# Strassen's scheme for the channel mixing of a hash-attention and MLP-mixer kernel

## The chip, the cores and the metric

The kernel runs on one core of a Trainium2 chip. The metric is the device time of one execution in microseconds. The engines are named as in the profile: PE is TensorE, which multiplies matrices out of SBUF into PSUM (PEld are its weight loads); DVE is VectorE; ACT is ScalarE; POOL is GpSimd; SP is SyncE, which issues most transfers.

## The reference

Attention in which a query sees only the keys of its own hash bucket (6 signs of a projection), then an MLP mixer: first over the tokens, then over the channels.

```python
q_bits = (np.einsum('bhsd,dk->bhsk', q, proj) > 0)      # k_bits likewise
mask = q_bucket[:, :, :, None] == k_bucket[:, :, None, :]
scores = np.where(mask, scale * np.matmul(q, k.transpose(0, 1, 3, 2)), -1000000000.0)
...
attn_out = softmax(scores) @ v                          # (4, 8, 768, 64)
x = attn_out.transpose(0, 2, 1, 3).reshape(4, 768, 512)
h = np.maximum(x.transpose(0, 2, 1) @ w_tok1, 0.0) @ w_tok2     # token mixing, 768 -> 256 -> 768
u = x + h.transpose(0, 2, 1)
h2 = np.maximum(u @ w_ch1, 0.0) @ w_ch2                 # channel mixing, 512 -> 1536 -> 512
return u + h2
```

The four weight matrices come as float64; the rest is float32.

## The kernel before

Three stages run one after the other, with all results of attention and mixing kept in SBUF in one tile, XT: 128 partitions, 4 blocks of 128 channels, 4 x 768 = 3072 tokens. In every stage the instructions of an engine stand in the order of the code (`tc.manual_schedule()`).

**attention** loops over 16 pairs of heads and two halves of 384 queries (class Half). For each half PE makes scores for 6 blocks of 128 keys (L292, product of q and k, and one of the sign bits that sets the mask), ACT takes exponentials out of PSUM (L309), PE multiplies with v (`weigh`, L317), DVE and POOL add the exponentials (`add`, L375 to L382), PE sums over the partitions (L327), DVE takes reciprocals (L329), POOL writes XT (L331). Once for each pair, `hashes` makes the next pair's signs: PE L265 into a small PSUM tile (tag "sm", one buffer, shared with the sums of L327), DVE L270 and L273 out of it, and 8 small transfers. `add_values` (ACT, L256) scales and sums the transposed v, tile vt. In the same loop `weights.some` converts a third of a 768-column piece of float64 weights at a time (class Conversion: ACT L164 and L194, DVE L166, L169, L181 and L195, POOL L184 and L185).

**mixer**, first part, mixes the tokens for each of the 4 batches: PE turns XT (`turn`, L225, copied by ACT), multiplies with w_tok1 (L526, out through ACT) and w_tok2 (L539), and DVE adds the result to XT (L545). Four PSUM buffers serve L526 and L539. After each of the two blocks of `mix1` and after each second channel block of `mix2` stands one call of `weights.one`, a whole conversion step: 16 places in all, for the second half of w_ch1 (tile WC1) and for w_ch2 (tile WC2).

**mixer**, second part, mixes the channels, 512 tokens at a time: `channels(tt)` makes 12 hidden blocks of 128 channels from 4 products each (L555, out through ACT, L560) and 4 output blocks from 12 products each (L565, DVE adds XT at L569, SP sends the result out at L570). `look` reads q and k again and takes their largest magnitude (L577), four pairs after each of four blocks of tokens; `decide` turns the 16 maxima on PE (L586) and leaves a flag. If the flag says that the values are large, a careful version of all stages runs afterwards; with these inputs it doesn't.

## Time and profile before

| | us |
|---|---|
| median of 3 runs | 968.51 (967.71 to 970.48) |
| the profiled execution | 967.04, of it span 965.3 |
| PE / DVE / ACT / POOL busy | 932.7 / 425.4 / 279.8 / 214.3 |
| channel mixing, first to last product | 464.4 to 960.1 |
| mean granted clock of PE | 0.992 of full |

A row of a group of instructions reads: line, engine, operation, tile written <- tiles read, partitions x elements and type, count | busy time in us, mean ns of one | idle time of that engine just before them, and what ended most of it. A row of the timeline begins with the start and the length in us; what stands in brackets is the idle time before it and what ended it.

### The profile page before, as it was taken

To read this page: it belongs to the slowest core of one execution; us is meant where nothing else is said; L and a number is where in the kernel's file an instruction comes from. 1 tells how busy PE (TensorE), PEld (TensorE's weight loads), DVE (VectorE), ACT (ScalarE), POOL (GpSimd) and SP (SyncE) were. 2 spreads that over 40 slices of the span, in tenths; PEclk is the share of its full clock that TensorE was granted. 3 is DMA by queue.
4 is the path that set the end of the run, shared out by engine and by line. 5 is a ranking of instruction groups with operands and counts; after the bars stand their busy time and mean duration, and the time that the engine had idled before them with its cause. 6 is when DMAs were issued, how large, how long until landed. Compare 5 with 4: busy or idle time off the path is not lost.

```text
span 965.3 us, 9061 instructions
## 1 busy us (share of the span) xinstructions
PE 932.7 (97%) x3649; PEld 418.5 (43%) x3649; DVE 425.4 (44%) x351; ACT 279.8 (29%) x390; POOL 214.3 (22%) x120
## 2 busy tenths in 40 slices
PE   5999999999999997999999999999999999999997
PEld 2444444434444443555444444444444444444443
DVE  1689989999899784898100110030020002000000
ACT  3555656565556452442110010011001001100100
POOL 3256345534454333575000000000000000000000
PEclk8999999999999998999999999999999999999999
DMA  5222332332222110441000210030040003000000
GB/s 210 88 101 69 111 123 76 102 124 100 94 75 69 35 58 13 127 131 33 1 0 22 109 43 11 22 141 0 22 148 5 11 32 132 0 33 11 1 12 34
DMA packets 20512, 61.11 MB, mean 63 GB/s; under 512 B 2800, under 2 KB 4208, under 8 KB 20464
## 3 DMA queue, kind: packets, MB, share of 16 engines
q1 hardware_dynamic: 20248, 60.45, 18.2%
q8 instruction: 30, 0.49, 0.2%
q14 instruction: 18, 0.15, 0.1%
q10 hardware_dynamic: 216, 0.02, 0.0%
HBM read 53.48 MB, written 6.29 MB: 62 GB/s over the span
## 4 chain that ended last, share of the span: by engine, by line
PE 82%; DVE 10%; ACT 4%; issue 2%; DMA 1%; SPq 0%; DVEq 0%; ACTq 0%
PE c L565 26%; PE c L555 26%; PE sc L292 14%; PE acc L317 10%; PE sums L327 2%; ACT e L309 2%; DVE tmp L169 2%; PE t L526 2%; PE t L539 2%; DVE tmp L166 1%; DVE den L329 1%; DVE WC L195 1%; DVE esd L381 1%; DVE esd L379 1%; ACT raw L194 1%
## 5 line engine op out<-in xcount | busy, mean ns | idle before, releaser
L555 PE MATMUL c<-XT,WC 128*128 128x512 f32 x576 | 248.2, 592 | 0.0
L565 PE MATMUL c<-r,WC 128*128 128x512 f32 x576 | 248.2, 592 | 0.0
L569 DVE TENSOR_TENSOR o<-c,XT 128x512 f32<-128x512 f32 x24 | 16.6, 690 | 424.2 <-PE c L565 424.2
L309 ACT ACTIVATE e<-sc 128x768 f32<-128x768 f32 x192 | 153.9, 811 | 101.5 <-PE sc L292 100.9
L292 PE MATMUL sc<-qk 64*128 64x384 f32 x768 | 164.7, 508 | 5.6 <-ACT e L309 5.6
L565 PEld LDWEIGHTS c<-r,WC 128*128 128x128 f32 x576 | 109.4, 190 | 137.8 <-issue 137.8
L555 PEld LDWEIGHTS c<-XT,WC 128*128 128x128 f32 x576 | 109.4, 190 | 137.1 <-issue 136.8
L560 ACT ACTIVATE r<-c 128x512 f32<-128x512 f32 x72 | 43.0, 597 | 428.8 <-PE c L555 428.8
L317 PE MATMUL acc<-e,vn 128*64 128x384 f32 x768 | 137.9, 494 | 0.0
L292 PEld LDWEIGHTS sc<-qk 64*128 64x128 f32 x768 | 66.2, 190 | 74.0 <-issue 60.1
L329 DVE RECIPROCAL den<-sums 128x384 f32<-128x384 f32 x32 | 81.8, 2556 | 26.0 <-PE sums L327 26.0
L331 POOL TENSOR_TENSOR XT<-num,den 128x384 f32<-128x384 f32 x32 | 49.1, 1535 | 166.0 <-ACT e L309 150.0
L375 POOL TENSOR_TENSOR esa<-e 128x768 f32<-128x768 f32 x32 | 79.4, 2482 | 19.8 <-ACT e L309 19.8
L317 PEld LDWEIGHTS acc<-e,vn 128*64 128x64 f32 x768 | 49.5, 136 | 78.4 <-issue 69.2
L381 DVE TENSOR_TENSOR esd<-esd,e 128x768 f32<-128x768 f32 x32 | 75.5, 2360 | 1.1
L292 PE MATMUL sc<-bits 64*128 64x384 bf16 x384 | 63.4, 324 | 0.2 <-DMA bits<-g 0.2
L184 POOL TENSOR_TENSOR tmp<-tmp,raw 128x768 f32<-128x768 f32 x20 | 42.2, 2109 | 49.5 <-DVE tmp L181 19.4
L379 DVE TENSOR_TENSOR esd<-esd,e 128x768 f32<-128x768 f32 x32 | 50.1, 1565 | 2.8
L526 PE MATMUL t<-x,W 128*128 128x512 f32 x96 | 44.6, 623 | 2.7 <-DVE den L329 2.7
L539 PE MATMUL t<-W,r 128*128 128x384 f32 x128 | 42.3, 488 | 0.9 <-DVE XT L545 0.9
L185 POOL TENSOR_TENSOR tmp<-tmp 128x768 f32<-128x768 f32 x20 | 39.4, 1972 | 1.6
L577 DVE TENSOR_REDUCE largest<-seen 128x1 f32<-128x1536 f32 x16 | 28.0, 1753 | 26.0 <-DMA seen<-in_qk 25.1
(45 smaller groups left out, 414.0 us busy)
## 6 DMA issues: line engine op xcount, KB each, us to landing
raw<-in_moe_w_ch SPq DMA_DIRECT2D x16, 768.0 KB
seen<-in_qk SPq DMA_DIRECT2D x16, 768.0 KB
qk<-in_qk SPq DMA_DIRECT2D x15, 768.0 KB
vn<-in_v SPq DMA_DIRECT2D x16, 384.0 KB
vt<-in_vT SPq DMA_DIRECT2D x16, 384.0 KB
out<-o SPq DMA_DIRECT2D x24, 256.0 KB
raw<-in_moe_w_tok SPq DMA_DIRECT2D x4, 768.0 KB
bits<-g SPq DMA_DIRECT2D x124, 5.2 KB
```

Source lines behind the costliest of these rows:

```text
L292: nc.tensor.matmul(sc[c][:, i, :HALF], t[rows, 1, P * c : P * c + P], t[rows, 0, qs], start=first, stop=not first,)
L309: nc.scalar.activation(e, sc[c][:, :, :HALF], ACT.Exp, scale=SCALE)
L317: nc.tensor.matmul(acc[D * i : D * i + D, :HALF], vn[:, i, c], e[:, i], start=(c == 0), stop=(c == NR - 1),)
L329: nc.vector.reciprocal(den, ps[:, :HALF])
L331: nc.gpsimd.tensor_tensor(XT[:, hp, at : at + HALF], num, den, op=ALU.mult)
L375: nc.gpsimd.tensor_tensor(self.a, es[0], es[1], op=ALU.add)
L379: nc.vector.tensor_tensor(self.d, self.d, es[5], op=ALU.add)
L381: nc.vector.tensor_tensor(self.d, self.d, es[2], op=ALU.add)
L526: nc.tensor.matmul(ps, W1[:, r, P * j : P * j + P], x[:, r], start=(r == 0), stop=(r == NR - 1),)
L539: nc.tensor.matmul(ps[:, :HALF], r1[:, j, P * cb : P * cb + P], W2[:, j, HALF * half : HALF * half + HALF], start=(j == 0), stop=(j == NJ ...
L555: nc.tensor.matmul(ps, WC1[:, cb, P * t : P * t + P], XT[:, cb, sl], start=(cb == 0), stop=(cb == NCB - 1),)
L565: nc.tensor.matmul(ps, WC2[:, t, P * cb : P * cb + P], r2[t], start=(t == 0), stop=(t == NHT - 1),)
```

## The change

Channel mixing takes 1024 tokens at a time and splits each of its two matrix products into 2 x 2 blocks. Seven products of blocks take the place of eight (Winograd's form of Strassen's scheme); they are made of sums and differences of blocks, all in float32. The sums of the weights (SW1, SW2) are made once by DVE, in four more jobs among the conversion jobs of token mixing (`weight_sums`, `jobs`). The sums of the tokens (T, `inputs`) are made by DVE for each 1024 tokens.

A hidden block of 128 + 128 channels (`hidden`) takes products into four PSUM banks b0 to b3. ACT copies b0, b2 and b3 out (p1, p5, p7), further products are added into the same banks, and DVE and POOL add up the four results, which DVE rectifies in place (L628). All eight banks are two sets of the four. `outputs` does the same with w_ch2, with the differences of the hidden blocks made by DVE in place and in T. `look` stands once behind each hidden block (from the third of the first 1024 tokens), and `decide` behind the last.

In attention, `add_values(0)` moves behind the first scores, `add_values(n + 1)` to the other half, and `hashes(n + 1)` ahead of `weights.some`. The token weights and x0 move to a pool that is closed before channel mixing.

```diff
@@ attention
-        add_values(0)
...
                 now.scores(0)
+                if n == half == 0:
+                    add_values(0)
...
                 now.add(0)
+                if half == 1 and n + 1 < len(pairs):
+                    add_values(n + 1)
                 if half == 0 and n + 1 < len(pairs):
-                    add_values(n + 1)
+                    hashes(n + 1)
                 if n:
                     weights.some(third)
                     third = (third + 1) % 3
-                if half == 0 and n + 1 < len(pairs):
-                    hashes(n + 1)
                 now.weigh(0)
@@ token mixing (mixer becomes tokens; weights.one() becomes job())
+    def weight_sums(w, sums, first, second, low, high):
+        a00, a01 = w[:, first, low], w[:, second, low]
+        a10, a11 = w[:, first, high], w[:, second, high]
+        def early():
+            nc.vector.tensor_tensor(sums[:, 1], a00, a10, op=ALU.subtract)
+            nc.vector.tensor_tensor(a10, a10, a11, op=ALU.add)
+        def late():
+            nc.vector.tensor_tensor(sums[:, 0], a10, a00, op=ALU.subtract)
+            nc.vector.tensor_tensor(sums[:, 2], a01, sums[:, 0], op=ALU.subtract)
+        return [early, late]
...
+            return [
+                *[conversion.one] * (n1 + 1),
+                *weight_sums(WC1, SW1, ...),
+                *[conversion.one] * n2,
+                *weight_sums(WC2, SW2, ...),
+            ]
@@ channel mixing
+        def hidden(s, t, r):
...
+            x.product(0, lambda k: WC1[:, k, low], lambda k: XT[:, k, sl[0]], ks, True)
+            x.product(1, lambda k: WC1[:, KC + k, low], lambda k: XT[:, KC + k, sl[0]], ks, True)
+            x.product(2, lambda k: WC1[:, k, high], lambda k: T[:, k], ks, True)
+            x.product(3, lambda k: SW1[:, 1, k, low], lambda k: T[:, 2 * KC + k], ks, True)
+            p1 = x.copy(0, "p1")
+            nc.vector.tensor_tensor(r[:, 0], x.ps[1], p1, op=ALU.add)
+            p5 = x.copy(2, "p5")
+            x.product(0, lambda k: SW1[:, 0, k, low], lambda k: T[:, KC + k], ks, False)
+            p7 = x.copy(3, "p7")
+            nc.gpsimd.tensor_tensor(p7, p5, p7, op=ALU.add)
+            x.product(2, lambda k: SW1[:, 2, k, low], lambda k: XT[:, KC + k, sl[1]], ks, False)
+            x.product(3, lambda k: WC1[:, KC + k, high], lambda k: T[:, 3 * KC + k], ks, False)
+            u = x.copy(0, "u")
+            nc.vector.tensor_tensor(r[:, 3], p7, u, op=ALU.add)
+            nc.vector.tensor_tensor(r[:, 1], x.ps[2], u, op=ALU.add)
+            nc.vector.tensor_tensor(r[:, 2], x.ps[3], u, op=ALU.add)
+            nc.vector.tensor_scalar(r, r, 0.0, None, op0=ALU.max)
...
+            nc.vector.tensor_tensor(t1, XT[:, low, b], XT[:, low, a], op=ALU.subtract)
+            nc.vector.tensor_tensor(t3, XT[:, high, b], XT[:, low, b], op=ALU.subtract)
+            nc.vector.tensor_tensor(t2, XT[:, high, b], t1, op=ALU.subtract)
+            nc.vector.tensor_tensor(t4, XT[:, high, a], t2, op=ALU.subtract)
...
+        inputs(0)
+        waiting = judge
+        for s in range(B * S // (2 * TT)):
+            rs = []
+            for t in range(HC):
+                r = pool.tile([P, 4, TT], F32, name="r2", tag="r2", bufs=HC)
+                hidden(s, t, r)
+                rs.append(r)
+                if s or t > 1:
+                    look()
+                if waiting and not unseen:
+                    decide()
+                    waiting = False
+            outputs(s, rs)
```

In `outputs`, for each of two output blocks of 128 + 128 channels (m): products of 6 chunks into b0 and b1 of both blocks first, then into b2 and b3 of both, then further ones into b0, b2 and b3. `inputs(s + 1)` stands between the last two groups.

The order of the instructions at the places in question. In the first: DVE in attention, one half with the hashes of the next pair; g are the signs, tmp and raw the conversion, den the reciprocal. Before, and then now:

```order
L382 SCALAR_TENSOR_TENSOR esd<-esd,esa 128x768
L166 TENSOR_SCALAR tmp<-raw 128x768
L169 SCALAR_TENSOR_TENSOR tmp<-raw,tmp 128x768
L270 TENSOR_SCALAR g<-hp 128x384
L273 TENSOR_SCALAR g<-g,bitscale 128x384
L329 RECIPROCAL den<-sums 128x384
```

```order
L383 SCALAR_TENSOR_TENSOR esd<-esd,esa 128x768
L272 TENSOR_SCALAR g<-hp 128x384
L275 TENSOR_SCALAR g<-g,bitscale 128x384
L168 TENSOR_SCALAR tmp<-raw 128x768
L171 SCALAR_TENSOR_TENSOR tmp<-raw,tmp 128x768
L331 RECIPROCAL den<-sums 128x384
```

The two instructions on the signs now stand ahead of the conversion.

The second place is DVE at the end of token mixing, from its last two adds to XT on (t are the banks that PE filled). Before, and then now:

```order
L545 TENSOR_TENSOR XT<-t_3279,XT 128x384
L545 TENSOR_TENSOR XT<-t_3283,XT 128x384
L569 TENSOR_TENSOR o<-c_3371,XT 128x512
L569 TENSOR_TENSOR o<-c_3387,XT 128x512
L569 TENSOR_TENSOR o<-c_3403,XT 128x512
```

```order
L549 TENSOR_TENSOR XT<-t_3291,XT 128x384
L549 TENSOR_TENSOR XT<-t_3295,XT 128x384
L571 TENSOR_TENSOR SW_2867<-WC_2865 128x1536
L681 TENSOR_TENSOR T<-XT 128x1024
L572 TENSOR_TENSOR WC_2865<-WC_2865 128x6x256
L682 TENSOR_TENSOR T<-XT 128x1024
L575 TENSOR_TENSOR SW_2867<-WC_2865 128x1536
L683 TENSOR_TENSOR T<-XT,T 128x1024
L576 TENSOR_TENSOR SW_2867<-WC_2865,SW_2867 128x1536
L684 TENSOR_TENSOR T<-XT,T 128x1024
L617 TENSOR_TENSOR r_3320<-b_3322,p_3333 128x512
```

The four sums of w_ch2 and the first four sums of tokens stand there in turn, ahead of the first hidden block's adds.

The third place is PE around the turning of the maxima (judge). Before it stands ahead of the last 512 tokens, and now between the last hidden block of the last 1024 tokens and their outputs:

```order
L565 MATMUL c_4059<-r_4009,WC_2859 128x512
L586 MATMUL judge<-ident,top 1x128
L555 MATMUL c_4082<-XT,WC_89 128x512 x4
L555 MATMUL c_4089<-XT,WC_89 128x512 x4
L555 MATMUL c_4096<-XT,WC_89 128x512 x4
```

```order
L595 MATMUL b_4251<-T,SW_2866 128x512 x2
L595 MATMUL b_4253<-XT,SW_2866 128x512 x2
L595 MATMUL b_4254<-T,WC_91 128x512 x2
L705 MATMUL judge<-ident,top 1x128
L595 MATMUL b_4293<-r_4070,WC_2865 128x512
L595 MATMUL b_4293<-r_4106,WC_2865 128x512
```

On DVE the maxima of the looks now stand behind the adds of that hidden block:

```order
L626 TENSOR_TENSOR r_4250<-b_4253,u 128x512
L627 TENSOR_TENSOR r_4250<-b_4254,u 128x512
L628 TENSOR_SCALAR r_4250<-r_4250 128x2048
L696 TENSOR_REDUCE largest<-seen 128x1
L703 TENSOR_REDUCE top<-largest 128x1
L707 TENSOR_REDUCE one<-judge 1x1
```

The turning thus comes behind that block's last add, its rectifier and the last look; before, it came behind the last add of the 512 tokens ahead.

## The prediction

> **What bounds the kernel now.** I read the page's busy table, chain and costliest groups first, then the time windows by stage, the table of waits, and the timeline at the places that the edits touch.

> ```profile
> span 965.3 us, 9061 instructions
> PE 932.7 (97%) x3649; PEld 418.5 (43%) x3649; DVE 425.4 (44%) x351; ACT 279.8 (29%) x390; POOL 214.3 (22%) x120
> PE 82%; DVE 10%; ACT 4%; issue 2%; DMA 1%; SPq 0%; DVEq 0%; ACTq 0%
> L555 PE MATMUL c<-XT,WC 128*128 128x512 f32 x576 | 248.2, 592 | 0.0
> L565 PE MATMUL c<-r,WC 128*128 128x512 f32 x576 | 248.2, 592 | 0.0
> ```

> TensorE (PE) is busy 97% of the span and is 82% of the chain that ended last. Channel mixing is 248.2 + 248.2 = 496.4 us of it. The code issues 288 products at each line and the profile shows 576 records, so a 128x512 float32 product is two records: 496.4/576 = 0.862 us. (The mean of 592 ns is a latency; records overlap.) The windows of attention, token mixing and channel mixing (length, then PE, PEld, DVE, ACT, POOL busy, clock, DMA) show the same by stage:

> ```profile
> 60.00:340.00 280.00, 273.73 (x1774) 117.64 (x1772) 254.39 (x187) 163.60 (x224) 130.88 (x67) 1.00 0.27 90
> 380.30:464.40 84.10, 81.30 (x274) 45.57 (x273) 69.05 (x73) 32.10 (x39) 49.13 (x23) 1.00 0.27 85
> 464.40:960.10 495.70, 494.81 (x1154) 218.59 (x1152) 44.98 (x43) 43.00 (x72) 0.00 (x0) 1.00 0.10 38
> ```

> Channel mixing has no gap but one of 0.9 us, and VectorE (DVE) is busy 45 of 496 us: there is cover for sums. In token mixing DVE is at 82%, in attention at 91%.

> **The products.** Per 1024 tokens there are 6 hidden blocks x 7 products x 2 chunks and 2 output blocks x 7 x 6, 168 instead of 192; three times that is 504 instead of 576. 72 x 0.862 = **62.1 us less** on PE.

> **The block sums.** The nearest rows:

> ```profile
> L569 DVE TENSOR_TENSOR o<-c,XT 128x512 f32<-128x512 f32 x24 | 16.6, 690 | 424.2 <-PE c L565 424.2
> L545 DVE TENSOR_TENSOR XT<-t,XT 128x384 f32<-128x384 f32 x32 | 16.3, 550 | 6.1 <-PE t L539 6.1
> L381 DVE TENSOR_TENSOR esd<-esd,e 128x768 f32<-128x768 f32 x32 | 75.5, 2360 | 1.1
> 361.56 0.96 DVE L381 TENSOR_TENSOR esd<-esd,e 128x768 f32<-128x768 f32 x1
> L181 DVE TENSOR_SCALAR tmp<-tmp 128x768 uint32<-128x768 uint32 x12 | 6.7, 560 | 0.4
> L577 DVE TENSOR_REDUCE largest<-seen 128x1 f32<-128x1536 f32 x16 | 28.0, 1753 | 26.0 <-DMA seen<-in_qk 25.1
> L560 ACT ACTIVATE r<-c 128x512 f32<-128x512 f32 x72 | 43.0, 597 | 428.8 <-PE c L555 428.8
> L185 POOL TENSOR_TENSOR tmp<-tmp 128x768 f32<-128x768 f32 x20 | 39.4, 1972 | 1.6
> ```

> 550 ns for 384 and 690 for 512 make 1.09 ns per element: 1.25 us for 1024, 1.81 for 1536 (768 would be 0.97, and L381 shows 0.96 when GpSimd, POOL, is idle; its mean of 2.36 is beside POOL's adds). The rectifier over 2048 is 0.56 x 2048/768 = 1.49.
> A hidden block takes PE 14 x 0.862 = 12.1 us. Under it DVE does 4 x 0.69 + 1.49 + a look at q and k 1.75 = 6.0 us, ScalarE (ACT) 4 copies x 0.6 = 2.4, POOL one add, some 1.4 us. PE adds again into a bank only after its copy: the bank that is written first is reopened after three other products (5 us) against 0.6 for the copy, so no wait. The output stage gives PE 84 x 0.862 = 72.4 us; DVE has 24 subtractions, 12 adds (36 x 0.69 = 24.8) and the next four sums of 1024 (5.0), 30 us. Subtractions of one half are needed 20.7 us (24 products) after their inputs, and 12 pairs take 16.6. I cost all of this at nothing, on PE's cover; without it each hidden block costs PE what DVE needs beyond 12.1 us. SyncE's output transfers come four per pair of blocks instead of one per block; none holds a buffer that is wanted within 12 us.

> **The moves in attention.** add_values(0) leaves the head of ACT's queue; the signs of the hashes (L270) pass the weight conversion in DVE's queue. The table of waits (total, times, longest), the timeline and the GB/s of each microsecond from 0:

> ```profile
> PE sums L327 <- DVE g L270: 6.7, 8, 1.3
> ACT vt L256 <- DMA vt<-in_vT: 14.1, 1, 14.1
> 11.47 0.95 PE L292 MATMUL sc<-bits 64*128 64x384 bf16 x6 [0.19 <-DMA bits<-g]
> 17.16 2.19 ACT L309 ACTIVATE e<-sc 128x768 f32<-128x768 f32 x3
> 18.00 1.65 PE L292 MATMUL sc<-qk 64*128 64x384 f32 x4 [5.58 <-ACT e L309]
> 22.12 0.85 PE L265 MATMUL hp<-qk,projblk 128*32 128x384 f32 x8
> GB/s 0 0 83 353 346 8 0 0 0 0 16 11 16 138 409 424 375 390 418 388 399 438 424 390 412 119 27 5 5 11 5 0 0 184 369 227 6 0 0 0
> 261.17 0.96 DVE L195 SCALAR_TENSOR_TENSOR WC<-raw,tmp 128x768 f32<-128x768 f32 x1 [1.08 <-ACT raw L194]
> 262.05 0.55 DVE L270 TENSOR_SCALAR g<-hp 128x384 bf16<-128x384 f32 x1
> 262.65 0.87 PE L327 MATMUL sums<-esd,ones 128*64 128x384 f32 x4 [1.25 <-DVE g L270]
> ```

> The scores are ready near 12, but ACT stood behind vt until 17.16. Now the three exponentials go first and PE resumes near 12.9. What is late next is q and k of pair 1 for L265: 2 x 384 KB stand ahead of its 768 KB, and the rates from 13 on (138, 409, 424, 375, 390) reach 1.57 MB at 17.6, some 0.7 more to land; L265 starts near 18.3 instead of 22.1. Bounds 0 (later transfers slow it) and 5.7 (it is there at 16.4); I take **3.5 us less**. The 8 waits of 6.7 us are PE waiting for the one small PSUM buffer until L270 has read it, behind L195 or L166 and L169. With L270 ahead they go: behind it now stands the conversion, which the reciprocal waits for, and the reciprocal feeds only POOL, with time. SyncE gets the hash transfers before the weight fetch, which nothing awaits soon. Bounds 3 and 6.7; I take **6.5 less**.

> **Token mixing.** Its slots, 16, now carry 17 jobs (13 conversion steps, four pairs of weight sums). DVE runs late here already:

> ```profile
> 442.23 2.09 DVE L166 TENSOR_SCALAR tmp<-raw 128x768 uint32<-128x768 uint32 x1
> 444.35 2.46 DVE L169 SCALAR_TENSOR_TENSOR tmp<-raw,tmp 128x768 uint32<-128x768 uint32 x1
> 447.32 0.95 DVE L195 SCALAR_TENSOR_TENSOR WC<-raw,tmp 128x768 f32<-128x768 f32 x1
> 448.19 1.94 DVE L545 TENSOR_TENSOR XT<-t,XT 128x384 f32<-128x384 f32 x4
> 448.80 15.75 PE L539 MATMUL t<-W,r 128*128 128x384 f32 x48 [0.74 <-DVE XT L545]
> 464.38 6.17 PE L555 MATMUL c<-XT,WC 128*128 128x512 f32 x14
> ```

> L545's adds stood behind a conversion step (442.23 to 448.2), and PE's next products waited 0.74 us for them at 448.80. Such a step takes 4.5 to 6 us, a pair of sums 3.6 (5.6 beside POOL). The first two pairs (slots 6 and 7) put 9 us in the place of 10.5, so DVE reaches 442 some 2 us earlier; but then two full steps fall between the last adds of L545, where DVE was idle. Walking both queues through the four banks, PE loses about 1.4 us at the last banks. Bounds 0 and 5; I take **1 more**.

> **Entry to channel mixing.** Behind the last L545 add DVE has four weight sums and the first four token sums in turn: 1.81 and 1.25, so that, counted from PE's last product of token mixing and with that add's 0.55, T is complete by quarters at 3.6, 6.7, 9.7 and 12.8 us. PE has two products (3.4 us) that need none; the next three (1.72 each) wait for a quarter each and end at 5.3, 8.4 and 11.4, one that needs none ends at 13.2, and the last at 14.9 instead of 12.1. **2.9 more**; bounds 1 (PE arrives late) and 5 (the last conversion on POOL runs beside them).

> **The judge.** The 16 looks are now one per hidden block, and the last stands behind hidden block 6 of the third pair. PE's transposition (L586 before, L705 now) is queued right behind that block and ahead of all outputs.

> ```profile
> 876.58 0.69 DVE L569 TENSOR_TENSOR o<-c,XT 128x512 f32<-128x512 f32 x1 [9.61 <-PE c L565]
> 877.19 0.16 DVE L584 TENSOR_REDUCE top<-largest 128x1 f32<-128x16 f32 x1
> 877.40 0.27 PE L586 MATMUL judge<-ident,top 128*1 128x128 f32 x1 [0.86 <-DVE top L584]
> 363.73 0.87 PE L327 MATMUL sums<-esd,ones 128*64 128x384 f32 x4 [2.59 <-DVE esd L382]
> 367.33 13.17 PE L526 MATMUL t<-x,W 128*128 128x512 f32 x24 [2.74 <-DVE den L329]
> 384.62 10.46 PE L526 MATMUL t<-x,W 128*128 128x512 f32 x24
> 14.00:15.00 1.00, 0.00 (x0) 0.00 (x0) 0.00 (x0) 0.00 (x0) 0.00 (x0) 0.62 1.05 409
> ```

> PE must wait for the last add 0.69, the rectifier 1.49, the look 1.75, a reduction of 0.16 and four handovers, together 4.3 us, 0.86 of which was paid before: 3.4 more. Such a gap also costs clock: after gaps of 2.59 and 2.74 us the same 24 records took 13.17 instead of 10.46 us, and at the start the granted clock fell to half by 14.2 (0.62 is the mean of that slice), 1.8 us after PE's last work ended at 12.4. I add 2.2 us (half clock for 3.4 to 6.8 us, part of it in the gap). **5.6 more**, bounds 2.5 and 7.
> [...]

> **The end and the sum.** The last add is again one of 512 behind the last product:

> ```profile
> 960.11 0.69 DVE L569 TENSOR_TENSOR o<-c,XT 128x512 f32<-128x512 f32 x1 [9.61 <-PE c L565]
> ```

> From its end, 960.8, to 965.3 lies the transfer, which stays. -62.1 - 3.5 - 6.5 + 1 + 2.9 + 5.6 = -62.6 us: span 965.3 to 902.7. The profiled execution was 967.04 us, 1.7 more than its span and 1.5 below the median of 968.51; 968.5 - 62.6 = **906 us**.

> **Rivals.**
> [...]
> - Attention keeps its time, because the reciprocal or the q and k of pair 1 now make PE wait as long: 906 + 10 = 916. For it: DVE at 91% there. Against it: the PSUM buffer is what the wait names.
> - Token mixing becomes DVE's: its 69 us in 84 grow by 4 pairs x 3.6 = 14.5, at POOL's pace 20; if a half of that lands on PE, 916.
> - DVE bounds the channel blocks in part: at L381's 2.5-fold pace the SBUF-only add and the rectifier make 6.0 into 9.3 us, still under 12.1; but if copies, POOL and DVE run one after the other at each block, 1 to 2 us x 18 are lost: 925 to 940. [...]
> - Slower: the same mechanism beyond its point. 62.6 us over 18 hidden blocks is 3.5 each, so DVE would need 15.6 us per block, 2.6 times my count; it gives 970 and more. No row shows all of DVE's work at that pace.
> - The compiled order could still issue the eighth product: 968. The built program has 504 products, against it.

> **Chances.** Forecast 0.57, clock holds 0.15, attention keeps its time 0.08, token mixing 0.10, partial bound by DVE 0.07, slower 0.02, no effect 0.01. A difference under 0.3% could not be told from none: faster 0.96, same 0.02, slower 0.02. Adding the good ends of the bounds to -62.1 (-5.7, -6.7, 0, +1, +2.5) gives 898; the attention and token cases end at 916 and their sums somewhat above: range 898 to 919, which leaves out the partial bound, slower and no effect.

> **What would show it.** Right: 1008 records of 512 columns at 0.43 us in channel mixing with waits only in its first block and at the judge; PE waiting about 4.3 us for the reduction of the looks, and the clock under 1.0 behind it; no wait of L327 for the signs; first exponentials near 12 us. Wrong: waits of PE on ACT copies or DVE adds in every block, or on token mixing's adds for over 5 us.

## The result and the profile after

The changed kernel takes 907.25 us (median of 4 runs, 905.23 to 907.36) against 968.11 us for the kernel before on the same chip: a ratio of 0.9363, 95% interval 0.9341 to 0.9384. The forecast was 906. Its profiled execution has a span of 905.5 us, 59.8 less than before. The busy line and the same windows by stage as before (the third is channel mixing behind its first hidden block up to the judge, the fourth from there to the last product):

```profile
span 905.5 us, 9108 instructions
PE 873.4 (96%) x3505; PEld 391.5 (43%) x3505; DVE 580.9 (64%) x545; ACT 293.4 (32%) x414; POOL 266.5 (29%) x156
...
60.00:340.00 280.00, 279.05 (x1808) 120.13 (x1806) 258.01 (x189) 167.07 (x228) 134.45 (x68) 1.00 0.25 87
374.28:459.02 84.74, 81.24 (x273) 45.54 (x272) 71.59 (x77) 32.16 (x39) 49.33 (x23) 1.00 0.28 93
473.56:826.12 352.56, 348.65 (x814) 154.09 (x812) 159.92 (x184) 49.23 (x84) 39.70 (x29) 1.00 0.13 46
826.12:900.20 74.08, 74.07 (x169) 32.41 (x169) 25.20 (x37) 4.69 (x8) 7.63 (x6) 0.98 0.07 26
```

PE is still the bound, with 59 us less work. In the attention window its idle time went from 6.3 us to 1.0. In the third window PE is idle for 3.91 us of 352.56, all of it one wait, while DVE is now busy 45% of the window. The table of PE's waits (total, times, longest) names what is left, here without four rows: the first products' wait for projblk (5.9 us, before 6.0), two waits that are as before (1.9 us at L227, 2.7 at L530), and one of 0.7 us of L294 for ACT's exponentials:

```profile
PE hp L267 <- DMA qk<-in_qk: 4.7, 1, 4.7
PE judge L705 <- DVE top L703: 3.9, 1, 3.9
PE sums L329 <- DVE esd L383: 3.4, 3, 2.6
PE t L543 <- DVE XT L549: 1.6, 2, 0.8
PE b L595 <- DVE T L683: 0.9, 1, 0.9
PE b L595 <- DVE T L682: 0.8, 1, 0.8
```

The wait of the sums (L329) for the signs is no longer there. The wait for q and k of the second pair of heads (its index is 1), 4.7 us at the hash products L267, is new. The timeline of the start, with the GB/s of each microsecond from 0:

```profile
12.18 2.21 ACT L311 ACTIVATE e<-sc 128x768 f32<-128x768 f32 x3 [9.94 <-PE sc L294]
20.45 1.51 PE L267 MATMUL hp<-qk,projblk 128*32 128x384 f32 x8 [4.72 <-DMA qk<-in_qk]
21.89 3.71 PE L319 MATMUL acc<-e,vn 128*64 128x384 f32 x12
34.85 0.81 PE L329 MATMUL sums<-esd,ones 128*64 128x384 f32 x4
...
GB/s 0 0 89 375 321 5 0 0 0 4 12 11 16 233 409 200 197 283 332 416 387 408 434 423 418 365 185 73 12 5 0 0 0 55 344 338 49 0 0 0
```

The exponentials do start at 12.18 instead of 17.16, yet the first sums come at 34.85, later than before (34.31, below). Then the entry to channel mixing, the judge, and the last add:

```profile
459.02 3.60 PE L595 MATMUL b<-XT,WC 128*128 128x512 f32 x8
465.44 1.98 PE L595 MATMUL b<-T,SW 128*128 128x512 f32 x4 [0.76 <-DVE T L682]
468.34 1.95 PE L595 MATMUL b<-T,SW 128*128 128x512 f32 x4 [0.91 <-DVE T L683]
473.56 1.88 PE L595 MATMUL b<-XT,WC 128*128 128x512 f32 x4
...
822.97 1.23 DVE L628 TENSOR_SCALAR r<-r 128x2048 f32<-128x2048 f32 x1
824.12 1.75 DVE L696 TENSOR_REDUCE largest<-seen 128x1 f32<-128x1536 f32 x1
825.89 0.17 DVE L703 TENSOR_REDUCE top<-largest 128x1 f32<-128x16 f32 x1
826.12 0.27 PE L705 MATMUL judge<-ident,top 128*1 128x128 f32 x1 [3.91 <-DVE top L703]
826.23 27.61 PE L595 MATMUL b<-r,WC 128*128 128x512 f32 x60
...
900.23 0.69 DVE L673 TENSOR_TENSOR u<-b,u 128x512 f32<-128x512 f32 x1 [4.46 <-PE b L595]
```

The first hidden block takes 473.56 - 459.02 = 14.54 us where the others take 12.02. In front of the judge PE waits for the rectifier, the look and the maxima, 3.15 us of DVE's work in a row. Then the 60 records behind it take 27.61 us, which take 25.91 in the runs without a fall of the clock (below): 0.43 us each, as in the third window, whose clock is 1.00.

### The profile page after: what moved, and what is told of

It is laid out like the page before. It is cut to its first block, busy times and chain, and to the rows that moved or that the text cites. A ratio compares the mean times of both kernels' runs of the same rounds, so it can differ in the third digit from the quotient of the medians.

```text
span 905.5 us, 9108 instructions
## 1 busy us (share of the span) xinstructions
PE 873.4 (96%) x3505; PEld 391.5 (43%) x3505; DVE 580.9 (64%) x545; ACT 293.4 (32%) x414; POOL 266.5 (29%) x156
## 4 chain that ended last, share of the span: by engine, by line
PE 88%; DVE 8%; DMA 1%; ACT 1%; issue 1%; POOL 0%; SPq 0%; DVEq 0%; ACTq 0%
PE b L595 47%; PE sc L294 16%; PE acc L319 13%; PE t L530 4%; PE sums L329 2%; PE t L543 2%; PE hp L267 2%; DVE den L331 1%; DVE esd L382 1%; DMA qk<-in_qk 1%; DVE esd L379 1%; DVE esd L380 1%; DVE tmp L171 1%; DVE XT L549 1%; DVE WC L197 1%; PE trp L227 1%
## 5 line engine op out<-in xcount | busy, mean ns | idle before, releaser
L294 PE MATMUL sc<-qk 64*128 64x384 f32 x768 | 163.6, 506 | 0.7 <-ACT e L311 0.7
L602 ACT COPY p<-b 128x512 f32<-128x512 f32 x72 | 42.2, 586 | 301.2 <-PE b L595 301.2
L319 PE MATMUL acc<-e,vn 128*64 128x384 f32 x768 | 139.5, 499 | 0.0
L595 PE MATMUL b<-r,WC 128*128 128x512 f32 x288 | 127.3, 599 | 0.0
L595 PE MATMUL b<-T,SW 128*128 128x512 f32 x216 | 97.0, 593 | 1.7 <-DVE T L683 0.9
L621 POOL TENSOR_TENSOR p<-p,p 128x512 f32<-128x512 f32 x18 | 25.5, 1414 | 238.8 <-ACT p L602 238.8
L294 PEld LDWEIGHTS sc<-qk 64*128 64x128 f32 x768 | 65.7, 188 | 68.7 <-issue 58.7
L595 PEld LDWEIGHTS b<-r,WC 128*128 128x128 f32 x288 | 55.2, 192 | 69.5 <-issue 67.6
L319 PEld LDWEIGHTS acc<-e,vn 128*64 128x64 f32 x768 | 50.0, 138 | 80.0 <-issue 71.2
L382 DVE TENSOR_TENSOR esd<-esd,e 128x768 f32<-128x768 f32 x32 | 75.5, 2361 | 1.1
L625 DVE TENSOR_TENSOR r<-p,u 128x512 f32<-128x512 f32 x18 | 12.5, 693 | 87.5 <-ACT u L602 87.0
L595 PE MATMUL b<-T,WC 128*128 128x512 f32 x144 | 67.7, 593 | 0.1
L595 PE MATMUL b<-XT,WC 128*128 128x512 f32 x144 | 64.7, 592 | 0.0
L595 PEld LDWEIGHTS b<-T,SW 128*128 128x128 f32 x216 | 40.9, 190 | 54.0 <-issue 50.7
L294 PE MATMUL sc<-bits 64*128 64x384 bf16 x384 | 63.2, 323 | 0.0
L595 PE MATMUL b<-r,SW 128*128 128x512 f32 x144 | 62.8, 592 | 0.0
```

The costliest lines, as they stand in the source:

```text
L294: nc.tensor.matmul(sc[c][:, i, :HALF], t[rows, 1, P * c : P * c + P], t[rows, 0, qs], start=first, stop=not first,)
L319: nc.tensor.matmul(acc[D * i : D * i + D, :HALF], vn[:, i, c], e[:, i], start=(c == 0), stop=(c == NR - 1),)
L382: nc.vector.tensor_tensor(self.d, self.d, es[2], op=ALU.add)
L595: nc.tensor.matmul(self.ps[i], left(k), right(k), start=first and k == ks[0], stop=k == ks[-1], skip_group_check=True,)
L602: nc.scalar.copy(c, self.ps[i])
```

## The experiments

Each kernel is the changed one with the edit shown. Ratios are to the kernel before on the same chip; where none is given, there is one run. Theory A is the reading above, B the rival.

**The judge's turning behind everything.**

```diff
                 if waiting and not unseen:
-                    decide()
+                    top = decide()
...
+        if judge:
+            turn_top(top)
```

> PE's turning of the maxima stands behind all outputs; DVE's reduction (L703) stays behind the last look. Theory A (the gap in front of the outputs costs its own 3.9 us and about 1.8 us of half clock behind it): no wait and no drop of the granted clock there, span 905.5 - 5.7 - 0.3 = about 899.5 us. Rival B (the outputs would wait anyhow for the last block's rectifier, so that only the wait's name changes): 904 to 905 us, with a wait of PE for the rectifier in its place.

Measured 902.58 us, ratio 0.9323 (0.9308 to 0.9339), span 901.4. The 60 records follow the hidden blocks without a gap and at full clock; 3.9 + 1.7 us are gone, as A says, and B's 904 to 905 is not seen. But only 4.1 us of the span went, because the end grew. The last rows:

```profile
822.02 25.91 PE L595 MATMUL b<-r,WC 128*128 128x512 f32 x60
...
894.12 0.27 PE L708 MATMUL judge<-ident,top 128*1 128x128 f32 x1
894.33 0.69 DVE L673 TENSOR_TENSOR u<-b,u 128x512 f32<-128x512 f32 x1 [4.46 <-PE b L595]
895.24 0.14 DVE L711 TENSOR_SCALAR unsafe<-one 1x1 int32<-1x1 f32 x1
```

The flag is now written last of all, and from the last product's end to the span's end lie 7.3 us instead of 5.3. What can't be read here is why a turning of 0.27 us and a flag of 0.14 us cost 2 us; the ninth run, which has both earlier, tests whether it is these two.

**The second weight sums later,** behind the first two hidden blocks instead of in the last slots of token mixing:

```diff
+                if judge and s == 0 and t < 2:
+                    weight_sums(WC2, SW2, ...)[t]()
...
                 *[conversion.one] * n2,
-                *weight_sums(WC2, SW2, ...),
```

> The four sums of w_ch2 leave the entry of channel mixing and stand behind the first and the second hidden block in DVE's queue. Theory A (PE waits in the first block because the weight sums stand between the four quarters of T): the first block takes 12.0 instead of 14.5 us, span about 903.0. Rival B (the quarters of T are late by themselves, or the later weight sums delay the next blocks): 905 to 906.

Measured 904.03 us, ratio 0.9344 (0.9327 to 0.9361), span 902.5. The first and the second hidden block:

```profile
458.14 3.60 PE L595 MATMUL b<-XT,WC 128*128 128x512 f32 x8
470.16 3.60 PE L595 MATMUL b<-XT,WC 128*128 128x512 f32 x8
```

12.02 us, as every other block: the 2.5 us at the entry were the four weight sums ahead of the four token sums in DVE's queue.

**The first weighing ahead of the hashes of the next pair,** at the start alone:

```diff
-                if half == 0 and n + 1 < len(pairs):
+                if half == 0 and 0 < n < len(pairs) - 1:
                     hashes(n + 1)
...
                 now.weigh(0)
+                if n == half == 0:
+                    hashes(1)
```

> For the first half of the first pair PE weighs v before it makes the hash products of pair 1, so the wait for q and k of pair 1 (4.7 us from 15.7 to 20.45) has 2 to 2.5 us of work in it. Theory A (the start lost its gain because PE stood behind that transfer, with the clock halved): products of the hashes still start near 20.4, but the work behind them comes 2 to 4 us earlier and the first sums (L329) start near 31.5 instead of 34.85; span about 902. Rival B (DVE and ACT behind the hashes set the pace of the start): the first sums stay within 0.5 us of 34.85, span 905.5.

Measured 904.14 us, ratio 0.9342 (0.9326 to 0.9357). The profiled execution, with a span of 900.4, is the fastest of four; the others have 902.2 to 902.6:

```profile
20.27 0.85 PE L267 MATMUL hp<-qk,projblk 128*32 128x384 f32 x8 [2.43 <-DMA qk<-in_qk]
30.37 0.81 PE L329 MATMUL sums<-esd,ones 128*64 128x384 f32 x4
```

q and k land no earlier, but PE has work meanwhile and the clock stays full (1.00 in each 0.2 us from 4.0 to 23.2; L267 takes 0.85 us for 1.51): the first sums come 4.5 us earlier. So it is the transfer that PE waits for, and with it the clock. In this execution the clock held at the judge too (see the last section).

**Attention in its old order** (`add_values` and `hashes` back where they stood), the channel mixing new:

```diff
+        add_values(0)
...
-                if n == half == 0:
-                    add_values(0)
...
-                if half == 1 and n + 1 < len(pairs):
-                    add_values(n + 1)
                 if half == 0 and n + 1 < len(pairs):
-                    hashes(n + 1)
+                    add_values(n + 1)
...
+                if half == 0 and n + 1 < len(pairs):
+                    hashes(n + 1)
```

> The three moves in attention are undone; channel and token mixing stay as changed. Theory A (the places add up: 6.4 us came from the hashes ahead of the conversion, and the start cost 0.5): the 8 waits of the sums for the signs are back, 6.7 us; span about 911.4. Rival B (the waits were shifted, not removed): span 905 to 907.

Measured 914.52 us, ratio 0.9438 (0.9416 to 0.9461). The profiled execution, with a span of 915.1, is the slowest of four (the fastest has 910.0). The waits for the signs are back to the digit, and a slow start beside them:

```profile
PE sums L329 <- DVE g L272: 6.7, 8, 1.3
PE sc L294 <- ACT e L311: 6.1, 1, 6.1
...
369.59 13.48 PE L529 MATMUL t<-x,W 128*128 128x512 f32 x24 [2.74 <-DVE den L331]
```

Token mixing's second products begin at 369.59; in the changed kernel (L530) at 361.46. Of these 8.1 us, 6.7 are the waits; and the first sums come at 35.90, 1.05 later than in the changed kernel and 1.6 later than in the kernel before, whose order this is: the start differs from run to run.

**Only `add_values(0)` back at the head of ACT's queue:**

```diff
+        add_values(0)
...
-                if n == half == 0:
-                    add_values(0)
```

> Only add_values is put back to its old places, ahead of ACT's first exponentials; the hashes stay ahead of the conversion. Theory A (the exponentials 5 us earlier bought nothing, since the hash products of pair 1 stand behind its q and k): first sums of PE between 34.0 and 34.9 us, span 905 to 906. Rival B (the forecast's: the earlier exponentials were worth 3.5 us and something else took them): first sums near 38, span near 909.

Measured 906.74 us in one run, span 905.0; the first sums at 34.26. So that move, for which the forecast took 3.5 us off, gave nothing in these runs: in the six profiles whose attention is that of the changed kernel, the first sums lie between 33.82 and 34.85.

**The rectifier four times in a row, and seven times,** which adds DVE work of 3 and 6 x 1.23 us to each of the 18 blocks and changes no value (`for _ in range(4):`, `range(7)`):

> The rectifier of each hidden block is made four times over (in place, same values): DVE has 2.8 + 4.9 + 1.75 = 9.4 us per block instead of 5.7, PE 12.0. Theory A (DVE is under PE's cover in the blocks; only what stands behind the last block of a pair shows): no waits in the blocks; outputs wait 0.69 + 4.9 - 4.3 = 1.3 us at each of two pairs and 3.7 longer at the judge: span 905.5 + 6 to 9 = 911 to 915. Rival B (the blocks are a chain of copies, adds and products, so each us on DVE shows): 18 x 3.7 = 66 us more, 970.

> The rectifier seven times over: DVE has 2.8 + 8.6 + 1.75 = 13.1 us per block, 1.1 more than PE's 12.0. Theory A: DVE falls behind by 1.1 us per block, PE waits only at the outputs, for the last rectifier: 0.7 + 8.6 + 5.7 - 4.3 = 10 to 11 us for each pair of blocks of tokens, and half clock behind; span 905.5 + 30 to 40 = 936 to 946. Rival B (chain): 18 x 7.4 = 133 more, 1038.

Measured 913.78 and 953.76 us in one run each. The waits of PE that are new or longer, first with four and then with seven:

```profile
PE judge L706 <- DVE top L704: 7.7, 1, 7.7
PE b L595 <- DVE r L629: 3.1, 2, 1.5
```

```profile
PE b L595 <- DVE r L629: 24.0, 3, 11.1
PE judge L706 <- DVE top L704: 20.3, 1, 20.3
```

With four, DVE has 4 x 0.69 + 4 x 1.23 + 1.75 = 9.4 us under a block of 12.02: 66 us more of DVE's work cost 6 to 7, all of it at the ends of the three pairs of token groups, where the outputs need the last block rectified. With seven it has 13.1, and PE waits 44 us, at the same three places and for what DVE has fallen behind. My expectation for seven (936 to 946) left out that the judge's pair pays for the rectifiers, the lag and the look together, and what its gaps of 10 to 20 us cost in clock (a mean of 0.966). B, an addition of all the work to the time, is wrong by far in both.

**q and k of the second pair ahead of v of the first:**

```diff
-        load_v(0)
         load_qk(1)
+        load_v(0)
```

> q and k of pair 1 are fetched ahead of v of pair 0. Theory A (transfers are served nearly in the order of their issue, so that q and k of pair 1 came last of three): the hash products of pair 1 start at 17.5 to 18.5 instead of 20.45, vt comes later and ACT's second exponentials with it; first sums 1 to 3 us earlier, span 902.5 to 904.5. Rival B (the rate of the transfers at the start sets the time, whatever the order): hash products at 19.5 to 20.5, span 905 to 906.

Measured 900.84 us in one run, span 899.0:

```profile
16.40 0.85 PE L267 MATMUL hp<-qk,projblk 128*32 128x384 f32 x8 [0.64 <-DMA qk<-in_qk]
29.66 0.81 PE L329 MATMUL sums<-esd,ones 128*64 128x384 f32 x4
...
GB/s 0 0 80 357 335 18 0 0 0 3 13 11 16 240 381 375 323 409 387 362 384 428 430 393 418 226 14 5 5 130 375 283 0 0 0 0 144 399 243 0
```

The first sums come 5.2 us earlier than in the changed kernel, more than A expected. The rest of the 6.5 us is the judge's clock, which held in this run (see the last section).

**The looks one block earlier, the turning one block behind them,** so that neither PE nor the end waits:

```diff
-                if s or t > 1:
+                if s or t > 0:
                     look()
                 if waiting and not unseen:
-                    decide()
+                    top = decide()
                     waiting = False
+                elif judge and not waiting:
+                    turn_top(top)
```

> The looks at the gaps of the weights are made from the second hidden block of the first pair on, the maxima of the look right behind the last of them, in the third pair, and TensorE's turning of those maxima behind block 6 of that pair, where the vector engine is long done; the flag is written then too, so nothing of it is left for the end. Theory A (the gap before the judge's turning costs its 3.9 us of waiting and 1.7 us of half clock, and the 2 us that came back when the turning stood last were the flag's, written too late): span 905.5 - 3.9 - 1.7 = 899.9, no clock fall near 827, the end 5.3 us behind the last product, median about 901.6. Rival B (the tail of 7.3 us has another cause than the flag, or the looks only move their wait to the pairs' ends): span 901.5 to 904, a wait of PE for the vector engine at one of the products of the hidden pairs.

Measured 901.34 us, ratio 0.9322 (0.9308 to 0.9337), span 898.5 in the profiled execution and 898.6 to 901.0 in the others, against 899.9 expected:

```profile
812.76 0.17 DVE L703 TENSOR_REDUCE top<-largest 128x1 f32<-128x16 f32 x1
...
820.93 0.27 PE L708 MATMUL judge<-ident,top 128*1 128x128 f32 x1
821.04 25.91 PE L595 MATMUL b<-r,WC 128*128 128x512 f32 x60
```

The maxima are ready 8 us ahead of the turning, the records run at full clock, and the end is 5.2 us long again. The 5.6 us of gap and clock go entirely, and the 2 us that came back in the first run came with the late turning and flag; which of the two it is, and why, stays open.

**Three edits together:** the judge as in this run, the sums later, q and k of the second pair first.

> Three edits at once: the judge's looks early as in the run beside it, the weights' second sums behind the first hidden block, and q and k of the first pair loaded ahead of the other transfers. Theory A (the three gaps lie in different places and nothing follows from one to the next): they add, 905.5 - 5.6 - 2.5 - 5.2 = 892.2 for the span, median about 894. Rival B (the start is set by the rate at which the transfers come, which is not the kernel's to choose, and the 5.2 us were a good draw of it): 892.2 + 2.5 to 5, a span of 895 to 897, with first sums of the attention later than 31.5 us.

Measured 894.34 us (5 runs, 893.44 to 895.16), ratio 0.9247 (0.9235 to 0.9260), span 891.4 in the profiled execution and 892.4 to 893.2 in the others, against 892.2 expected: the gains add, B's 895 to 897 is not seen. It is the fastest of these kernels, 1.4% below the changed one.

## Why the prediction was right, and where it was not

The first and the last but one sums of attention, in the kernel before and now, fix what the loop took; the row of the scores (L292) is the kernel before at half clock:

```profile
19.76 1.46 PE L292 MATMUL sc<-qk 64*128 64x384 f32 x4
...
34.31 0.81 PE L327 MATMUL sums<-esd,ones 128*64 128x384 f32 x4
...
355.62 0.81 PE L327 MATMUL sums<-esd,ones 128*64 128x384 f32 x4
```

```profile
349.75 0.81 PE L329 MATMUL sums<-esd,ones 128*64 128x384 f32 x4
```

- **Products**, -62.1: channel mixing is 900.18 - 459.02 = 441.16 us against 495.69; without the entry and the judge that is 61.8 less. A product takes 0.858 us; no block waits inside.
- **Start of attention**, -3.5: measured +0.5. This is the step that failed. The forecast took the transfer rates of the old trace (424, 375, 390 GB/s from 15 us on) to place q and k at 18.3; they were 200, 197 and 283, and L267 started at 20.45, 1.7 us earlier than before and not 3.8. The rate is only half of that: with the new rates the forecast's own count (1.57 MB from 13 us on, and 0.7 us to land) comes to about 19.4, an estimate from the GB/s row. (The 0.7 fits vt in the kernel before: the 0.79 MB up to it had moved by 15.6, and ACT's wait for it ended at 16.32.) The other 1.0 us lies in the count or in the landing, and the run with the later sums shows it at faster rates (last section). So PE's idle time was exchanged, 0.70 + 4.72 us for 5.58, and not removed. Half clock followed both gaps (granted 0.50 from 14.23 to 21.06 us before, from 18.23 to 25.06 now): L267 and L319 now took 1.51 and 3.71 us for 0.85 and 2.16, 2.2 more, while the scores behind the old gap (1.65 and 1.46 us for 0.92 and 0.81, and the sign products between them) had lost 1.6. The bound "0 (later transfers slow it)" was too kind, since it left out the clock that the new gap costs. The third, fifth and eighth run show from three sides that it is this transfer.
- **Waits for the signs**, -6.5: the loop took 321.31 us before and 349.75 - 34.85 = 314.90 after, -6.4; put back, they are 6.7 us again.
- **Token mixing**, +1: 84.74 us against 84.04, +0.7, in two waits of 0.76 and 0.85 us for the adds of L549. The rival in which DVE's sums bound it, 916, falls.
- **Entry**, +2.9: +2.5, by the queue that was named.
- **Judge**, +5.6: 3.91 - 0.86 + 1.70 = +4.8. The gap was 4.3 in the forecast because the rectifier was priced at 1.49 us by another operation's row; it took 1.23 (1226 to 1229 ns in all 18). The 2.2 us for the clock were an estimate, from half clock for 3.4 to 6.8 us; this run shows half clock for 3.41 us (827.19 to 830.60), which cost 1.7. That the clock fell at all, 1.7 of the 4.8, was a draw (last section). One of the four executions has a span of 903.4 at a mean clock of 0.992, the others 905.4 to 905.6 at 0.989 to 0.990; it may have been spared the fall, which no trace shows.
- **The end**, 0: 5.3 us in both.

The measured terms add up to -61.8 + 0.5 - 6.4 + 0.7 + 2.5 + 4.8 = -59.7, and the span fell by 59.8. The forecast's -62.6 was 2.8 too good. The start alone was 4.0 too good; the judge, the entry and token mixing, priced 0.8, 0.4 and 0.3 too high, made up for a part of it. That the median came out only 1.25 us above 906 is luck beyond that: the forecast went from a median 1.5 us above the profiled execution, and of the changed kernel the two are the same. The rivals by DVE's pace fall with the run of four rectifiers: 3.7 us more per block did not reach PE's products.

## What to carry to other kernels

Fewer products on a saturated TensorE came through almost whole, 61.8 of 62.1 us, because the added sums fitted, block by block, under the products; what decides is the slack per block and what stands at the few places where a later stage needs the last block at once. What is moved off a queue's head gains nothing until what is late next is also moved: price that by its landing time, and price the gap in PE with the clock that it can cost (here 2.2 us behind the gap of 4.72 at the start). A reduction whose result is needed at some time later should be finished a block early: last in line it cost 4.8 us (1.7 of them by the clock), at the very end 2, and one block early nothing.

## What the runs showed of the hardware

```profile
823.76:827.17 3.41, 1.05 (x4) 0.57 (x5) 2.98 (x6) 0.00 (x0) 0.00 (x0) 1.00 0.00 0
827.17:830.58 3.41, 3.41 (x6) 1.33 (x5) 3.31 (x6) 0.00 (x0) 0.00 (x0) 0.50 0.00 0
```

```profile
10.82:14.23 3.41, 1.41 (x10) 0.30 (x6) 0.00 (x0) 0.00 (x0) 0.00 (x0) 1.00 0.32 77
```

```profile
10.30:13.71 3.41, 1.63 (x10) 0.37 (x8) 0.00 (x0) 0.00 (x0) 0.00 (x0) 1.00 0.19 50
```

```profile
815.83:819.24 3.41, 1.49 (x4) 0.38 (x2) 2.35 (x4) 0.00 (x0) 0.00 (x0) 1.00 0.00 0
819.24:822.65 3.41, 1.42 (x5) 0.70 (x6) 2.95 (x7) 0.00 (x0) 0.00 (x0) 1.00 0.00 0
```

Windows busy 31%, 41% and 48% were followed by half clock (the last by the first slice of its profile, 22.9 us at under 0.8 of full clock, and by the scores at 18.44, which took 1.65 us for 0.92); in the run with q and k first an edge at 819.24, an estimate (136 windows behind the fall at 355.03), split the gap, both windows were 42 to 44% busy, and the clock held. Of six kernels with the gap of 3.91 us, four lost the clock behind it (the 60 records took 27.6 to 28.3 us), with 13 to 39% in the window ahead, and two, this one and the one that weighs first, did not (25.91), with 41 to 45%: two of six, where the forecast gave that rival a chance of 0.15. So whether the forecast or its rival "clock holds" came true went, in these six, with where the gap fell on the windows, about which the order of instructions says nothing. A limit on the busy share alone doesn't come out of these runs: at the judge falls and holds part near 40%, but at the start a window of 48% lost the clock while one of 42% at the judge kept it. What is counted stays open.

**The rate of the first transfers** is not the kernel's alone. In the microseconds from 15 to 18 the kernel before had 424, 375 and 390 GB/s. With the same transfers in the same order the changed kernel had 200, 197 and 283, and the run with attention in its old order 277, 206 and 264; with q and k first it was 375, 323 and 409 in one run and 369, 252 and 344 in the three edits together. So the forecast took a good draw for the rule. But the rate isn't all that made q and k late. The run with the later sums, whose attention is that of the changed kernel, had rates nearer to the old ones:

```profile
19.94 0.85 PE L267 MATMUL hp<-qk,projblk 128*32 128x384 f32 x8 [4.17 <-DMA qk<-in_qk]
...
GB/s 0 0 72 375 338 5 0 0 0 2 15 11 16 249 350 372 326 366 381 367 380 426 422 402 415 244 56 13 5 5 0 0 92 313 363 18 0 0 0 0
```

From 13 us on it had moved the forecast's 1.57 MB by about 17.7, and still L267 started 2.2 us later and not 0.7. Where q and k were fetched first, the same estimate with their 0.79 MB leaves 1.0 us (15.4 to 16.40). Why it is longer behind the other transfers stays open: the count left out the fetches that were issued after q and k, and no run takes these away. The exponentials, earlier or later, are not what slows the rate, since they start late in the old order too (PE's wait for them ends at 18.44, in the changed kernel at 13.04); what does stays open.
